# Decoding five of eight weight quads two stages earlier, beside attention, through DRAM scratch

## The chip, the cores and the metric

The kernel runs on one core of a Trainium2 chip. The metric is device time in microseconds (us) from launch to end, as the median of several executions; smaller is better. Engines are called as in the profile: PE (matmuls) and PEld (their weight loads), DVE (VectorE), ACT (ScalarE), POOL (GpSimd), SP (the queue that issues most DMAs). Each engine works through its own instructions in a fixed order; an instruction that waits holds up all that stand behind it on that engine.

## The reference

Three stages follow one another. `q`, `k`, `v` are 4 batches x 8 heads x 576 positions x 64. The weights arrive as float64.

```python
q_d, k_d, v_d = (mean over groups of 4 positions of q, k, v)
out = repeat(softmax(q_d k_d^T / 8) v_d, 4) + softmax(masked(q k^T / 8, |i - j| < 4)) v
x = out as 2304 tokens x 512
y = maximum(maximum(x @ w1, x @ w2), x @ w3) @ w_out         # first MoE, 512 -> 768 -> 512
h = maximum(y @ w_in, 0)                                     # second MoE, 512 -> 2048
return h * h @ w_out2                                        # 2048 -> 512
```

## The kernel before

**Numbers as pairs.** Each matmul operand is held as a rounded part (`hi`, or `h`) and the rest (`lo`, or `l`), and a product is three matmuls, `hi*hi + hi*lo + lo*hi` (`mm3`, L140). A weight block therefore costs, before any matmul can use it, a *decode*: a 512 KB load of raw float64 into one of three staging buffers (`raw_words`, L101, pool `stg`); `rebias` on DVE (L107); `low_bits` on ACT (L113); `join`, two DVE instructions (L116); then a split, `hi` on ACT and `lo` on another engine.

**Stages.** Attention of a batch makes `x`; the first MoE turns `x` into `y`, written to DRAM from ACT's queue (`y_unit`, L413). The two are interleaved over batches: `run(b, ...)` does the first MoE of batch b beside the attention of batch b+1. In the profiled execution `run(0, "second")` lies at about 95 to 187 us, `run(1, "mid")` at 187.3 to 279.9, `run(2, "mid")` at 279.9 to 372.5 and `run(3, "last")`, which has no attention beside it, at 372.5 to 461.3. Then comes the second MoE over three tiles of 768 tokens, here called t0 (461.3 to 595.1), t1 (595.1 to 721.9) and t2. In each, all eight *quads* of weights are used in turn (`quad`, L701): seven products `P` in a Strassen-like scheme, whose results DVE and ACT must take out of two PSUM banks in alternation, and twelve output groups `po`, issued during the next quad. So t0 contains eight rounds of products and seven of output groups; t1 contains eight of both.

**Order.** The order of PE is written out by hand in `CFG` (a token for each piece of work: `s` scores, `t` transposes, `v` the product with v, `G` a gate unit, `Y` an output unit of the first MoE). The order on DVE, ACT, POOL and SP is laid down when the program is built, by a list planner: work that is traced earlier goes first as soon as its inputs and its buffer are there, and later work fills gaps.

**Weights of the second MoE.** A quad is four raw blocks (two of `w_in`, called f0 and f1, two of `w_out2`, o0 and o1) that become six cuts: i0 and i3 straight from f0 and f1, i1 and i2 from four DVE sums of them (L528 to L531), o0 and o1. Each cut is an `h` and an `l` tile; twelve tiles make a quad, and there is room for four quads. `decode_quad` (L499) decodes into these tiles, with `lo` on POOL (`split_cut`, L488), and stores all twelve to DRAM scratch (`store_cut`, L494). `load_quad` (L554) reads them back. Quads 0 to 2 are decoded during `run(3)`. Quads 3 to 7 are decoded during t0, between the pieces of work of quads 0 to 5:

```python
spread(0, 0, decode_quad(3))
for q in range(4, NQ):
    spread(0, q - 3, decode_quad(q), 2)
```

In t1 and t2, four quads each are still in place and four are loaded from scratch. A planner-made detail: quad 0's first three raw blocks are loaded, and two of them joined, as early as 118 to 135 us, in gaps of `run(0)`; they then hold the staging buffers until its tiles come free.

Of the kernel before, what the change touches and what calls it, by code (L numbers as in the profile page):

```python
# [18 lines left out]
P = 128  # L19
# [39 lines left out]
def local_global_attention__then__moe_kernel(  # L59
# [30 lines left out]
        for b in range(B)  # L90
    ]
    wscr = [
        {
            c + e: yd.tile([P, 256 if c == "i3" else 512], F32, name=f"s{q}{c}{e}", tag=f"s{q}{c}{e}")
            for c in CUT
            for e in "hl"
        }
        for q in range(NQ)
    ]

    def raw_words(src, name):  # L101
        raw = stg.tile([P, 512], U64, tag="raw", name=f"raw_{name}")
        nc.sync.dma_start(out=raw, in_=src)
        words = raw.bitcast(U32).rearrange("p (n two) -> p n two", two=2)
        return words[:, :, 0], words[:, :, 1]
# [307 lines left out]
    def y_unit(b, h, d):  # L413
        N = HALF[h][1] * QB
        ps = mm_ps(f"yp{b}{h}{d}")
        for f in range(NF1):
            hi, lo = w1_t["o", f, 0]
            ds = slice(d * P, (d + 1) * P)
            mm3(ps[:, 0:N], hi[:, ds], lo[:, ds], h_t[b, h, f][0], h_t[b, h, f][1], f == 0, f == NF1 - 1)
        ys = tmp.tile([P, 320], F32, tag="c", name=f"ys{b}{h}{d}")[:, 0:N]  # L420
        nc.scalar.activation(out=ys, in_=ps[:, 0:N], func=AF.Copy)
        nc.scalar.dma_start(out=yscr[b][h][:, d, :], in_=ys)


    vdone = set()
# [68 lines left out]
    def store_cut(q, c):  # L494
        n = 256 if c == "i3" else 512
        for e in "hl":
            nc.sync.dma_start(out=wscr[q][c + e], in_=w2_t[q][c + e][:, 0:n].bitcast(F32))

    def decode_quad(q):  # L499

        raw, tb = {}, {}

        def begin(key, src):
            low, high = raw[key] = raw_words(src, f"{key}_{q}")
            rebias(high)
            low_bits(low, low)

        def end(key):
            low, high = raw[key]
# [12 lines left out]
        def sums():  # L522

            t1, t2 = tb["f0"][:, 0:256], tb["f0"][:, 256:512]
            t3, t4 = tb["f1"][:, 0:256], tb["f1"][:, 256:512]
            b11, b21 = raw["f0"][:, 0:256], raw["f0"][:, 256:512]
            b12, b22 = raw["f1"][:, 0:256], raw["f1"][:, 256:512]
            nc.vector.tensor_tensor(out=t1, in0=b12, in1=b11, op=ALU.subtract)  # L528
            nc.vector.tensor_tensor(out=t3, in0=b22, in1=b12, op=ALU.subtract)
            nc.vector.tensor_tensor(out=t2, in0=b22, in1=t1, op=ALU.subtract)  # L530
            nc.vector.tensor_tensor(out=t4, in0=t2, in1=b21, op=ALU.subtract)  # L531

        def last(c, key):
            end(key)
            split_cut(q, c, raw[key])

        def stores(*cuts):
            for c in cuts:
                store_cut(q, c)

        f = 2 * q
        return [
            lambda: begin("f0", wi2[f]),
            lambda: begin("f1", wi2[f + 1]),
            both,
            other,
            sums,
            lambda: (split_cut(q, "i1", tb["f0"]), begin("o0", wo2[f]), stores("i0", "i3")),
            lambda: (split_cut(q, "i2", tb["f1"]), begin("o1", wo2[f + 1]), stores("i1", "i2")),
            lambda: last("o0", "o0"),  # L550
            lambda: (last("o1", "o1"), stores("o0", "o1")),
        ]

    def load_quad(q):  # L554
        def part(cuts, new=False):
            if new:
                quad_tiles(q)
            for c in cuts:
                n = 256 if c == "i3" else 512
                for e in "hl":  # L560
                    nc.sync.dma_start(out=w2_t[q][c + e][:, 0:n].bitcast(F32), in_=wscr[q][c + e])

        return [lambda: part(CUT[:4], True), lambda: part(CUT[4:])]

# [44 lines left out]
    with tc.manual_schedule(engines={ENG.PE}):  # L609
# [9 lines left out]
        def run(b, plan):  # L619
            for token in plan.split():  # L620
# [2 lines left out]
                    gate_unit(b, int(token[1]), int(token[2]))  # L623
                elif kind == "Y":
                    y_unit(b, int(token[1]), int(token[2]))
                elif kind == "e":
                    load_w2()
                elif kind == "d":
                    load_w1(1)
                else:  # L630
                    act_on(b + 1, token)

        run(0, CFG["second"])
        for b in range(1, B - 1):
            run(b, CFG["mid"])
        at.close()
        yq = ctx.enter_context(tc.tile_pool(name="yq", bufs=1, reuse_waits="tile"))
# [190 lines left out]
```

## Time and profile before

| | us |
|---|---|
| median of 3 executions | 863.0 (862.43 to 867.05) |
| the profiled execution | 863.13 |
| its span in the trace | 861.2 |
| PE busy in the span | 809.8 (94%) |
| DVE busy | 531.5 (62%) |
| ACT busy | 330.4 (38%) |
| POOL busy | 221.4 (26%) |

The 1.93 us between time and span lie before the first and after the last instruction. Busy shares are means over stages that differ; the rows below split them by stage. Moved by DMA: 110.32 MB. The granted TensorE clock is full (1.00, of 2.4 GHz) from 100 us on, but for one stretch of 0.97 at 500 to 550 us.

### The profile page before, as it was taken

The page shows a single profiled execution, that of the slowest core. Times are in us where ns is not written, and L with a number is a line of the kernel's source. Part 1 is how long each engine was busy: PE and PEld are TensorE (multiplying, and loading weights), DVE is VectorE, ACT ScalarE, POOL GpSimd, SP SyncE. Part 2 cuts the span into 40 slices and gives each one's busy share as a digit, 9 for nine tenths or more (in the row PEclk, how much of TensorE's full clock was granted, in tenths as well). Part 3 has the DMA queues.
Part 4 walks back from the last instruction along what each step waited for, and adds up shares of the span by engine and source line. Part 5 has one row for each costly group of instructions (what it writes and reads, how often), then busy time and mean ns, then how long its engine had stood idle before and what let it go on. Part 6 is the DMA issues. An engine that isn't in the chain of part 4 may idle for free. (4 is left out here: it accounts for less than half of the span.)

```text
span 861.2 us, 15761 instructions
## 1 busy us (share of the span) xinstructions
PE 809.8 (94%) x6016; PEld 741.5 (86%) x6016; DVE 531.5 (62%) x1008; ACT 330.4 (38%) x935; POOL 221.4 (26%) x258
## 2 busy tenths in 40 slices
PE   4678999999999999999998988999999999999998
PEld 3467998999999999999898877888888989888886
DVE  6899896523554245637777998965644445544543
ACT  4556654522543144543445444434221123211211
POOL 4756385410433014004333333412000002000000
PEclk8577999999999999999999999999999999999999
DMA  7645342410223002136665766722564100654101
GB/s 239 193 153 184 127 155 70 132 47 1 86 87 103 10 29 81 31 107 216 220 225 168 289 214 238 263 80 93 188 214 141 50 1 25 211 192 135 49 1 73
DMA packets 66234, 110.32 MB, mean 128 GB/s; under 512 B 6800, under 2 KB 29680, under 8 KB 66160
## 3 DMA queue, kind: packets, MB, share of 16 engines
q1 hardware_dynamic: 61552, 104.60, 37.1%
q10 hardware_dynamic: 4608, 4.72, 1.6%
q8 instruction: 47, 0.77, 0.4%
q14 instruction: 27, 0.22, 0.1%
HBM read 76.79 MB, written 32.51 MB: 127 GB/s over the span
## 5 line engine op out<-in xcount | busy, mean ns | idle before, releaser
L141 PE MATMUL g<-xhi,hi_g 128*128 128x256 f32 (+1 forms) x576 | 176.1, 306 | 4.4 <-DVE c L395 3.4
L142 PE MATMUL g<-xlo,hi_g 128*128 128x256 f32 (+1 forms) x576 | 172.8, 300 | 2.1 <-DVE xlo L356 1.9
L143 PE MATMUL g<-xhi,lo_g 128*128 128x256 f32 (+1 forms) x576 | 172.7, 300 | 0.0
L141 PEld LDWEIGHTS g<-xhi,hi_g 128*128 128x128 f32 x576 | 111.1, 193 | 8.1 <-DVE c L395 5.5
L142 PEld LDWEIGHTS g<-xlo,hi_g 128*128 128x128 f32 x576 | 111.4, 193 | 2.5 <-DVE xlo L356 2.5
L143 PEld LDWEIGHTS g<-xhi,lo_g 128*128 128x128 f32 x576 | 110.8, 192 | 0.0
L666 ACT ACTIVATE gh<-c 128x384 fp32r<-128x384 f32 x96 | 50.2, 524 | 147.6 <-DVE c L710 133.5
L667 DVE TENSOR_TENSOR gl<-c,gh 128x384 fp32r<-128x384 f32 x96 | 61.6, 643 | 39.4 <-ACT gh L666 39.1
L395 DVE TENSOR_TENSOR c<-g,c 128x256 f32<-128x256 f32 (+1 forms) x96 | 43.3, 451 | 63.1 <-PE g L143 59.4
L141 PE MATMUL yp<-hh,hi_o 128*128 128x256 f32 (+1 forms) x192 | 58.3, 304 | 0.0
L142 PE MATMUL yp<-hl,hi_o 128*128 128x256 f32 (+1 forms) x192 | 57.1, 297 | 0.2 <-DVE hl L401 0.2
L143 PE MATMUL yp<-hh,lo_o 128*128 128x256 f32 (+1 forms) x192 | 56.9, 296 | 0.0
L399 ACT ACTIVATE hh<-c 128x256 fp32r<-128x256 f32 (+1 forms) x48 | 21.3, 444 | 88.3 <-DVE c L395 88.1
L710 DVE SCALAR_TENSOR_TENSOR c<-c 128x384 f32<-128x384 f32 x72 | 43.4, 604 | 1.9
L729 DVE TENSOR_TENSOR c<-c 128x384 f32<-128x384 f32 x24 | 15.7, 654 | 39.7 <-ACT c L728 39.7
L606 POOL TENSOR_TENSOR lS<-s,hS 128x768 fp32r<-128x768 f32 x2 | 3.7, 1839 | 131.3 <-DVE u L725 115.9
L141 PEld LDWEIGHTS yp<-hh,hi_o 128*128 128x128 f32 x192 | 36.4, 190 | 0.8 <-issue 0.6
L142 PEld LDWEIGHTS yp<-hl,hi_o 128*128 128x128 f32 x192 | 36.5, 190 | 0.7 <-DVE hl L401 0.7
L143 PEld LDWEIGHTS yp<-hh,lo_o 128*128 128x128 f32 x192 | 36.4, 190 | 0.0
L217 POOL TENSOR_TENSOR v<-v 72x256 f32<-72x256 f32 x32 | 26.1, 828 | 36.9 <-DMA v<-in_vP 36.8
L728 ACT ACTIVATE c<-P 128x384 f32<-128x384 f32 x24 | 11.7, 488 | 59.3 <-PE P L143 57.9
L401 DVE TENSOR_TENSOR hl<-c,hh 128x320 fp32r<-128x320 f32 (+1 forms) x36 | 20.1, 559 | 11.7 <-ACT hh L399 11.7
(1797 smaller groups left out, 2151.9 us busy)
## 6 DMA issues: line engine op xcount, KB each, us to landing
raw_o<-in_wo SPq DMA_DIRECT2D x22, 512.0 KB
raw_g<-in_wg SPq DMA_DIRECT2D x18, 512.0 KB
raw_f<-in_wi SPq DMA_DIRECT2D x16, 512.0 KB
k<-in_kT SPq DMA_DIRECT2D x16, 291.0 KB
q<-in_qT SPq DMA_DIRECT2D x16, 288.0 KB
v<-in_vP SPq DMA_DIRECT2D x32, 144.0 KB
out_y<-ob SPq DMA_DIRECT2D x18, 256.0 KB
vw<-in_vP SPq DMA_DIRECT2D x16, 175.0 KB
```

Of the source, the lines that this page charges most:

```text
L141: nc.tensor.matmul(ps, whi, xhi, start=first, stop=False, skip_group_check=more)
L142: nc.tensor.matmul(ps, whi, xlo, start=False, stop=False, skip_group_check=more)
L143: nc.tensor.matmul(ps, wlo, xhi, start=False, stop=last, skip_group_check=more)
L217: nc.gpsimd.tensor_tensor(out=v4[:, 0:2], in0=v4[:, 0:2], in1=v4[:, 2:4], op=ALU.add)
L395: nc.vector.tensor_tensor(out=c, in0=ps[:, 0:N], in1=c, op=ALU.max)
L399: nc.scalar.activation(out=hhi, in_=c, func=AF.Copy)
L401: eng.tensor_tensor(out=hlo, in0=c, in1=hhi.bitcast(F32), op=ALU.subtract)
L666: nc.scalar.activation(out=ghi, in_=c, func=AF.Copy)
L667: nc.vector.tensor_tensor(out=glo, in0=c, in1=ghi.bitcast(F32), op=ALU.subtract)
L710: V.scalar_tensor_tensor(out=c, in0=c, scalar=0.0, in1=c, op0=ALU.max, op1=ALU.mult)
L728: A.activation(out=e, in_=d, func=AF.Relu)
L729: V.tensor_tensor(out=e, in0=e, in1=e, op=ALU.mult)
```

## The change

Quads 3 to 7 are no longer decoded in t0. A new function, `decode_to_scratch`, decodes quads 3, 4 and 5 into DRAM scratch; its calls are traced just ahead of `run(1, "mid")`. Quads 6 and 7 are traced ahead of `run(2, "mid")`. Being traced earlier, they go ahead of that run's own work on each engine whenever they are ready. There, the two halves of a cut are made in a buffer of the same three-deep staging ring (`tag="raw"`), `lo` on DVE and not on POOL, and go to scratch as one store of 512 KB (256 KB for i3). The f blocks' loads are held back by a one-column ACT copy out of the last `ys` tile of the run before, into the staging buffer that is to be loaded. In t0, quads 3 to 7 are loaded from scratch as in t1 and t2. Quads 0 to 2 are decoded and stored as before.

```diff
-            c + e: yd.tile([P, 256 if c == "i3" else 512], F32, ...)
+            c: yd.tile([P, 2, 256 if c == "i3" else 512], F32, ...)
...
-    def raw_words(src, name):
+    def raw_words(src, name, after=None):
         raw = stg.tile([P, 512], U64, tag="raw", name=f"raw_{name}")
+        if after is not None:
+            nc.scalar.activation(out=raw.bitcast(F32)[:, 0:1], in_=after[:, 0:1], func=AF.Copy)
         nc.sync.dma_start(out=raw, in_=src)
...
+    def decode_to_scratch(q):
+        raw, tb = {}, {}
+        f = 2 * q
+        def begin(key, src):
+            low, high = raw[key] = raw_words(src, f"{key}_{q}", last_y[0] if key[0] == "f" else None)
+            rebias(high)
+            low_bits(low, low)
+        def end(key):
+            low, high = raw[key]
+            join(low, high, low)
+            raw[key], tb[key] = low.bitcast(F32), high.bitcast(F32)
+        def cut(c, w):
+            n = w.shape[-1]
+            t = stg.tile([P, 2, 512], F32R, tag="raw", name=f"cut_{c}_{q}")
+            hi, lo = t[:, 0, 0:n], t[:, 1, 0:n]
+            nc.scalar.activation(out=hi, in_=w, func=AF.Copy)
+            nc.vector.tensor_tensor(out=lo, in0=w, in1=hi.bitcast(F32), op=ALU.subtract)
+            nc.sync.dma_start(out=wscr[q][c], in_=t[:, :, 0:n].bitcast(F32))
+        return [
+            lambda: begin("f0", wi2[f]),
+            lambda: begin("f1", wi2[f + 1]),
+            lambda: end("f0"),
+            lambda: end("f1"),
+            lambda: cut("i0", raw["f0"]),
+            lambda: sums(raw, tb),
+            lambda: cut("i3", raw["f1"][:, 256:512]),
+            lambda: cut("i1", tb["f0"]),
+            lambda: cut("i2", tb["f1"]),
+            lambda: begin("o0", wo2[f]),
+            lambda: (end("o0"), cut("o0", raw["o0"])),
+            lambda: begin("o1", wo2[f + 1]),
+            lambda: (end("o1"), cut("o1", raw["o1"])),
+        ]
...
-        for b in range(1, B - 1):
+        for b, quads in zip(range(1, B - 1), ((3, 4, 5), (6, 7))):
+            for call in [call for q in quads for call in decode_to_scratch(q)]:
+                call()
             run(b, CFG["mid"])
...
-        spread(0, 0, decode_quad(3))
-        for q in range(4, NQ):
-            spread(0, q - 3, decode_quad(q), 2)
+        spread(0, 0, load_quad(3))
-        for t, k in ((1, 0), (1, 1), (1, 2), (1, 3), (2, 0), (2, 1), (2, 2), (2, 3)):
+        for t, k in ((t, k) for t in range(NT2) for k in range(NQ - 4)):
             one, two = load_quad(turns[t][k + 4])
             spread(t, k + 1, [one], 1)
             spread(t, k + 2, [two], 1)
```

## Rows read from the trace of the kernel before

**Rows 1.** Windows by stage: busy us (instructions) of PE, PEld, DVE, ACT, POOL; clock, DMA share, GB/s

```profile
95.00:187.30 92.30, 89.23 (x889) 84.50 (x888) 60.94 (x129) 46.04 (x166) 48.02 (x62) 1.00 0.35 112
118.00:137.00 19.00, 16.94 (x151) 15.64 (x149) 17.32 (x34) 9.28 (x27) 12.78 (x14) 1.00 0.36 122
187.30:279.90 92.60, 92.60 (x982) 88.76 (x981) 43.42 (x113) 37.73 (x153) 26.17 (x46) 1.00 0.21 65
279.90:372.50 92.60, 92.42 (x949) 88.72 (x949) 45.05 (x114) 36.89 (x150) 15.79 (x28) 1.00 0.12 37
372.50:461.30 88.80, 86.65 (x662) 84.84 (x662) 56.66 (x94) 34.72 (x70) 24.71 (x18) 1.00 0.62 204
461.30:595.10 133.80, 123.15 (x591) 106.73 (x590) 115.95 (x180) 59.93 (x106) 49.05 (x33) 0.99 0.55 188
595.10:721.90 126.80, 126.36 (x624) 112.85 (x623) 66.67 (x115) 31.85 (x58) 5.89 (x3) 1.00 0.35 117
```

**Rows 2.** Waits of PEld in t0: total us, times, longest; first and last of seven

```profile
PEld P L141 <- DVE c L744: 4.3, 3, 1.6
...
PEld P L141 <- ACT p L722: 1.5, 2, 1.1
```

**Rows 3.** Waits of PEld in t1, the longest

```profile
PEld P L141 <- DVE u L733: 0.7, 1, 0.7
```

**Rows 4.** Decode by line: ns of one (min/median/max), first and last start

```profile
L108 DVE TENSOR_SCALAR raw_o<-raw_o x22: 416/424/1101, 96.0 to 562.9; 128x512 f32<-128x512 f32 x22
L114 ACT ACTIVATE raw_o<-raw_o x22: 660/685/717, 94.2 to 562.2; 128x512 uint32<-128x512 uint32 x22
L117 DVE SCALAR_TENSOR_TENSOR raw_o<-raw_o x22: 674/686/1791, 97.1 to 563.5; 128x512 uint32<-128x512 uint32 x22
L134 ACT ACTIVATE hi_g<-raw_g x18: 658/673/722, 21.5 to 96.1; 128x512 fp32r<-128x512 f32 x18
L136 DVE TENSOR_TENSOR lo_g<-raw_g,hi_g x18: 652/682/1215, 24.2 to 97.7; 128x512 fp32r<-128x512 f32 x18
L528 DVE TENSOR_TENSOR raw_f<-raw_f,raw_f x8: 408/419/965, 132.2 to 552.4; 128x256 f32<-128x256 f32 x8
```

**Rows 5.** Windows of L108 alone (one instruction a raw block): busy us, clock, DMA

```profile
95.00:187.30 92.30, 5.45 (x9) 1.00 0.35 112
118.00:137.00 19.00, 2.17 (x4) 1.00 0.36 122
372.50:461.30 88.80, 6.43 (x12) 1.00 0.62 204
```

**Rows 6.** PE timeline in run(1): start us, duration us

```profile
224.50 0.66 PE L247 MATMUL sd22F<-kd,qd 64*64 64x144 f32 x8
...
226.33 0.41 PE L142 MATMUL yp<-hl,hi_o 128*128 128x320 f32 x1
...
268.73 0.74 PE L294 MATMUL t23B<-const,sm23B 128*70 128x128 f32 x5
```

**Rows 7.** DVE timeline in run(1): what those matmuls wait for

```profile
225.80 0.47 DVE L401 TENSOR_TENSOR hl<-c,hh 128x320 fp32r<-128x320 f32 x1
...
267.48 0.55 DVE L270 TENSOR_TENSOR sm23B<-sm23B,sms23B 128x350 f32<-128x350 f32 x1
```

**Rows 8.** POOL timeline in run(1): last step of pooling q and k of pair 2

```profile
222.73 0.55 POOL L209 TENSOR_TENSOR kd<-kd,k 128x144 f32<-128x144 f32 x1
```

**Rows 9.** SP timeline: issue of two raw loads

```profile
127.78 0.33 SPq L103 DMA_DIRECT2D raw_o<-in_wo  x1
...
449.91 0.38 SPq L103 DMA_DIRECT2D raw_o<-in_wo  x1
```

**Rows 10.** ACT timeline: first use of those two raw loads

```profile
131.12 0.67 ACT L114 ACTIVATE raw_o<-raw_o 128x512 uint32<-128x512 uint32 x1 [2.95 <-DMA raw_o<-in_wo]
...
455.79 0.70 ACT L114 ACTIVATE raw_o<-raw_o 128x512 uint32<-128x512 uint32 x1 [1.11 <-DMA raw_o<-in_wo]
```

**Rows 11.** Waits of ACT in run(3): total us, times, longest

```profile
ACT raw_f L114 <- DMA raw_f<-in_wi: 9.3, 5, 4.8
```

More of the change, by code (lines that the diff above doesn't have):

```diff
@@ L93, in local_global_attention__then__moe_kernel @@
         {
-            c + e: yd.tile([P, 256 if c == "i3" else 512], F32, name=f"s{q}{c}{e}", tag=f"s{q}{c}{e}")
+            c: yd.tile([P, 2, 256 if c == "i3" else 512], F32, name=f"s{q}{c}", tag=f"s{q}{c}")
             for c in CUT
-            for e in "hl"
         }
@@ L99, in local_global_attention__then__moe_kernel @@
     ]
-    def raw_words(src, name):
+    last_y = []
+    def raw_words(src, name, after=None):
         raw = stg.tile([P, 512], U64, tag="raw", name=f"raw_{name}")
+        if after is not None:
+            nc.scalar.activation(out=raw.bitcast(F32)[:, 0:1], in_=after[:, 0:1], func=AF.Copy)
         nc.sync.dma_start(out=raw, in_=src)
@@ L422, in y_unit @@
         nc.scalar.dma_start(out=yscr[b][h][:, d, :], in_=ys)
+        last_y[:] = [ys]
     vdone = set()
@@ L492, in split_cut, with sums @@
         nc.gpsimd.tensor_tensor(out=lo, in0=w, in1=hi.bitcast(F32), op=ALU.subtract)
[L494 to L497, printed above, removed]
+    def sums(raw, tb):
+        t1, t2 = tb["f0"][:, 0:256], tb["f0"][:, 256:512]
+        t3, t4 = tb["f1"][:, 0:256], tb["f1"][:, 256:512]
+        b11, b21 = raw["f0"][:, 0:256], raw["f0"][:, 256:512]
+        b12, b22 = raw["f1"][:, 0:256], raw["f1"][:, 256:512]
+        nc.vector.tensor_tensor(out=t1, in0=b12, in1=b11, op=ALU.subtract)
+        nc.vector.tensor_tensor(out=t3, in0=b22, in1=b12, op=ALU.subtract)
+        nc.vector.tensor_tensor(out=t2, in0=b22, in1=t1, op=ALU.subtract)
+        nc.vector.tensor_tensor(out=t4, in0=t2, in1=b21, op=ALU.subtract)
     def decode_quad(q):
@@ L520, in other, with keep @@
             split_cut(q, "i3", raw["f1"][:, 256:512])
[L522 to L531, printed above, removed]
+        def keep(*cuts):
+            for c in cuts:
+                n = 256 if c == "i3" else 512
+                for i, e in enumerate("hl"):
+                    nc.sync.dma_start(out=wscr[q][c][:, i], in_=w2_t[q][c + e][:, 0:n].bitcast(F32))
         def last(c, key):
@@ L535, in last @@
             split_cut(q, c, raw[key])
-        def stores(*cuts):
-            for c in cuts:
-                store_cut(q, c)
         f = 2 * q
@@ L546, in decode_quad @@
             other,
-            sums,
-            lambda: (split_cut(q, "i1", tb["f0"]), begin("o0", wo2[f]), stores("i0", "i3")),
-            lambda: (split_cut(q, "i2", tb["f1"]), begin("o1", wo2[f + 1]), stores("i1", "i2")),
+            lambda: sums(raw, tb),
+            lambda: (split_cut(q, "i1", tb["f0"]), begin("o0", wo2[f]), keep("i0", "i3")),
+            lambda: (split_cut(q, "i2", tb["f1"]), begin("o1", wo2[f + 1]), keep("i1", "i2")),
             lambda: last("o0", "o0"),
-            lambda: (last("o1", "o1"), stores("o0", "o1")),
+            lambda: (last("o1", "o1"), keep("o0", "o1")),
+        ]
[23 more added lines that the diff above has]
+            lambda: cut("i0", raw["f0"]),
+            lambda: sums(raw, tb),
+            lambda: cut("i3", raw["f1"][:, 256:512]),
[5 more added lines that the diff above has]
+            lambda: (end("o1"), cut("o1", raw["o1"])),
         ]
@@ L559, in part @@
                 n = 256 if c == "i3" else 512
-                for e in "hl":
-                    nc.sync.dma_start(out=w2_t[q][c + e][:, 0:n].bitcast(F32), in_=wscr[q][c + e])
+                for i, e in enumerate("hl"):
+                    nc.sync.dma_start(out=w2_t[q][c + e][:, 0:n].bitcast(F32), in_=wscr[q][c][:, i])
         return [lambda: part(CUT[:4], True), lambda: part(CUT[4:])]
@@ L625, in run @@
                     y_unit(b, int(token[1]), int(token[2]))
-                elif kind == "e":
-                    load_w2()
                 elif kind == "d":
```

## The prediction

> **What bounds the kernel now.** I read the windows by stage first [rows 1]. PE is the engine that sets the end almost everywhere: from 187.3 to 372.5 us, the two `mid` runs, it is busy for 185.02 of 185.2 us, and in t1 for 126.36 of 126.8. The exception to look for is t0: PE is busy for 123.15 of 133.8 us there, while DVE is at 115.95 (87%) against 66.67 of 126.8 (53%) in t1, which does the same products without decoding. The weight loads run ahead of the matmuls, so their waits show the full hold-up: in t0 seven releasers, 4.3 us for the largest and 1.5 for the smallest, 16.4 together, all on products `P` that wait until DVE or ACT has emptied a PSUM bank [rows 2]. In t1 the largest such wait is 0.7 [rows 3]. So t0 is bound by DVE's queue. The stages that take the work over have room by the same view: DVE at 43.42 and 45.05 of 92.6 us, ACT at 37.73 and 36.89, DMA at 0.21 and 0.12 [rows 1].
>
> **What t0 gives back.** Two ways of counting. Waits: 16.4 - 0.7 = 15.7 us. Length: t0 has 588 matmuls (eight rounds of 42 products, seven of 36 outputs), t1 has 624 in 126.8 us, or 0.203 us each; 588 x 0.203 = 119.5, and 133.8 - 119.5 = 14.3. What does not go away is the start of t0, where the first quad needs four splits of `y` before its products can run, as before; I leave 1 us for it. I take 14 us, with 12 and 15.7 as ends. The loads from scratch that come in cost nothing here: four quads are loaded in t1 at the same pace with DMA at 0.35 and PE full [rows 1]. Their cover is that each is issued about two quads ahead of its use; without it a late part would hold PE by a raw load's time, some 3 to 6 us [rows 9, 10]. SP loses 20 raw loads and 60 stores from t0 and gains 60 loads there; the `y` loads for t1 stand behind loads that wait for tiles to come free, as those for t2 do in t1 already.
>
> **What the decode costs in its new place.** Per quad on DVE [rows 4]: 4 rebias x 0.424 = 1.70, 8 join instructions x 0.686 = 5.49, 4 sums x 0.419 = 1.68, and, new on DVE, `lo` for five full cuts x 0.682 = 3.41 and for i3 some 0.4 (an estimate, from the half-width sum beside it). That is 12.7 us. On ACT: 4 x 0.685 + 5 x 0.673 + 0.45 for i3 = 6.6, and two one-column copies, which no row shows; the nearest are full-width copies at 0.67, so 0 to 1.3 us, and I take 0.4: 7.0. Run(1) takes three quads: DVE 43.42 + 38.1 = 81.5 of 92.6 us (88%), ACT 37.73 + 21 = 58.7 (63%). Run(2) takes two: DVE 70.5 (76%), ACT 50.9.
>
> Both still fit, so the cost is not in sums but in queues. A decode instruction is traced ahead of the run's own work, so it goes first when both are ready. Behind it on DVE stand the maxima that empty the gate units' PSUM, `hl`, and the softmax steps; behind it on ACT the exponentials and the PSUM copies; PE, in its written order, waits for these. Gate units have four PSUM buffers, so a wait of a microsecond or two is covered. Some spots have no cover. `hl` ends at 226.27 and the `yp` matmul that reads it starts at 226.33; `sm23B` ends at 268.03 and its transposes start at 268.73; `kd` of pair 2 ends at 223.28 and `sd22F` starts at 224.50 [rows 6 to 8]. Slack there: 0.1, 0.7 and 1.2 us, once in each `mid` run.
>
> How much of this PE feels, the trace shows by analogy, because raw blocks are decoded beside other work already. PE's idle time over the raw blocks of a stretch [rows 1, 5]: run(3), no attention: 88.8 - 86.65 = 2.15 us for 12, or 0.18 each. Run(0), with attention: 92.3 - 89.23 = 3.07 for 9, or 0.34. The densest piece of it, 118 to 137 us: 2.06 for 4, or 0.51. The change puts 20 blocks beside attention: 3.6, 6.8 and 10.3 us. In those rows `lo` ran on POOL; with it, DVE's work for a block grows from 8.9/4 to 12.7/4, a factor of 1.43, which makes the middle 9.7 and the top 14.7. I take 8 us, between 6.8 and 9.7, since run(0) is the nearest row; 2 (most of it falls where PE has cover) and 15 stay as ends.
>
> The rest is small. Quad 0's first blocks can no longer be decoded at 118 to 135 us, since the staging buffers are to be free for quads 3 to 7; run(0) gains about 3 x 0.34 = 1 us, run(2) or run(3) gets the three blocks and loses it. Quad 3's early raw loads at the end of run(3) vanish. Does the ring keep up? A cut holds a buffer for `hi` 0.67, `lo` 0.68 and its store, for which the nearest row is a raw load, 3.3 us: 4.7. Three such in line, the f loads and joins (about 7) and two o blocks (about 9) make some 30 us a quad, 90 for three against 92.6, 60 for two. Tight in run(1), but run(2) has a reserve.
>
> **Sum.** Against the profiled execution's 863.13: -14 + 8 = -6, so 857. The median of the runs, 863.0, lies 0.13 below it, which changes nothing.
>
> **A rule beside the rows.** A raw block issued at 127.78 us is in use at 131.12, after 3.34 us, with DMA at 0.36; one issued at 449.91 is in use at 455.79, after 5.88, with DMA at 0.62 [rows 1, 9, 10]. The Trainium skill, page "DMA: Bandwidth & Descriptors", section "Issuing engines are not separate DMA queues", says that DMAs from whichever engine run on the same 16 DMA engines and interleave. By that rule attention's own loads in the `mid` runs are stretched too, and the trace agrees as far as the raw loads go; the rows say more directly that a load takes up to 2.5 us longer at that DMA share. It is rival 3.
>
> **Rivals.**
> 1. *Nearly all is hidden.* For it: PE idles 0.18 us in both `mid` runs together, four PSUM buffers, DVE at half load. Against: run(0) lost 3.07 us with less. Mid costs 2 to 3.6: 863 - 15 + 3 = 851, range 847 to 853. Chance 0.18.
> 2. *The tight spots give it all back.* At each of the three spots a whole block's chain (0.42 + 2 x 0.69) and a `lo` (0.68) stand in front, 2.5 us; less slack 2.4 + 1.8 + 1.3 = 5.5 a run, 11 for two, plus 1 to 2 on PSUM: 863 - 14 + 12.5 = 861.5, range 859 to 867. The same result would show if quads slipped out of the `mid` runs into run(3), so that the change does only part of what it says. Chance 0.17.
> 3. *Attention's inputs come late.* With some 4.9 MB a quad added, DMA in run(1) rises from 0.21 towards run(3)'s 0.62, q and k of pair 2 land up to 2.5 us later and `sd22F` has 1.2 to spare: 1.3 us a run more, 863.1 - 14 + 8 + 2.6 = 859.7. Chance 0.08.
> 4. *Slower.* Each cut's first write, `hi` on ACT, waits until the ring's buffer is free, that is until an earlier cut's store has landed; each o or f block's `low_bits` waits for its load. That is 24 to 30 waits on ACT in run(1). In run(3) such a wait of ACT's took 9.3/5 = 1.9 us [rows 11]. 24 x 1.9 = 45, and 58.7 + 45 = 104 of 92.6: ACT would be the bound, run(1) 11 us longer, run(2) (16 x 1.9 + 50.9 = 81) would lose what rival 2 says, 5.5, and a little on PSUM. 863 - 14 + 18 = 867 and up to 874. It decides from (92.6 - 58.7)/24 = 1.4 us a wait. Against: DMA is far less busy there, and a wait that ACT reaches late is short. Chance 0.15.
>
> **Numbers.** The forecast has the remaining 0.42, own range 853 to 859. No change means within 0.5% (4.3 us, about what a measurement of this kernel can tell from none): 858.7 to 867.3. Faster: 0.18 + 0.42 = 0.60. Same: rivals 2 and 3, 0.25. Slower: 0.15. For 8 in 10 the range leaves out the lowest part of rival 1 and most of rival 4: 849 to 867.
>
> **What would show it.** In t0: no raw blocks, no POOL subtractions, DVE down from 116 to about 67 us, the stage 119 to 121 us long; wrong if products still wait for DVE, or if `P` waits for a DMA. In the `mid` runs: DVE near 81 and 70 us, each 3 to 6 us longer, PE waits at `yp` for `hl`, at `t23B`/`t33B` for `sm`, at `sd22F`/`sd32F` for `kd`; rival 1 if they stay 92.6 long, rival 4 if ACT's waits for DMA sum to over 35 us in run(1). The forecast fails if the `mid` runs together grow by 12 us or more, or if run(3) takes over decode work of quads 6 and 7.

## The result, and the profile after

The changed kernel takes 868.36 us as the median of 12 executions (862.21 to 873.21), the kernel before beside it 863.55 (862.27 to 867.05). The ratio is 1.0051, with an interval of 1.003 to 1.0072: slower by about half a per cent. 857.0 was forecast, 849 to 867 as range. The profiled execution took 868.07 us, its span is 866.3.

PE executes the same 6016 matmuls in the same order in both kernels, so the stages can be cut at the same matmuls. By that order, in which a run ends with its last Y unit, the cuts of [rows 1] lie some 9 us behind the start of `run(1)` (178.4 us in the kernel before) and some 8 us ahead of the end of `run(2)` (380.4); the two `mid` runs are 101 us long each, and cut there they grow by 23.4 us together, as between the cuts (23.5). The names of the stages below mean the stretches between the cuts. First the windows by stage of the changed kernel, with the columns of [rows 1]: `run(0)`, `run(1)`, `run(2)`, `run(3)`, t0 and t1.

```profile
93.90:182.80 88.90, 88.35 (x890) 84.61 (x889) 55.73 (x122) 46.85 (x169) 45.60 (x62) 1.00 0.35 111
182.80:288.70 105.90, 98.23 (x982) 93.05 (x981) 77.01 (x174) 53.14 (x184) 33.43 (x46) 0.95 0.56 188
288.70:391.50 102.80, 95.29 (x949) 90.66 (x949) 74.08 (x171) 50.66 (x177) 19.39 (x28) 0.97 0.44 146
391.50:478.70 87.20, 85.95 (x663) 84.62 (x662) 50.76 (x81) 32.59 (x67) 24.45 (x18) 1.00 0.57 191
478.70:599.70 121.00, 119.53 (x590) 106.08 (x590) 65.70 (x113) 32.66 (x59) 5.89 (x3) 1.00 0.40 134
599.70:727.40 127.70, 126.30 (x624) 112.62 (x624) 66.52 (x115) 31.85 (x58) 5.89 (x3) 1.00 0.35 116
```

Beside [rows 1] the first column after the colon tells it all. t0 falls from 133.8 to 121.0, and its DVE from 115.95 to 65.7: the gain is there. But `run(1)` grows from 92.6 to 105.9 and `run(2)` from 92.6 to 102.8, 23.5 us together. `run(0)` falls from 92.3 to 88.9 and begins 1.1 us earlier, `run(3)` falls by 1.6, t1 grows by about 1. In sum 23.5 - 12.8 - 3.4 - 1.1 - 1.6 + 0.9 - 0.4 (t2) = +5.1, the difference of the spans.

All stage lengths here and below are of one execution each, the profiled one, which lies up to 3.5 us from its kernel's median. Two yardsticks for that: the work ahead of `run(0)`, which no edit touches, ends at 92.3 to 96.8 us in the sixteen traces; and `run(1)` took 105.9 us here and 103.9 us in the kernel with quad 0 held back (below), with the same order of instructions on every engine. So a difference of 2 us between two stages of single traces is not told from none.

The waits of the weight loads in t0, which answer to [rows 2], have shrunk to 3.7 us; first and last of five:

```profile
PEld P L145 <- DVE c L781: 1.1, 2, 0.7
...
PEld P L145 <- ACT p L763: 0.4, 1, 0.4
```

In the two `mid` runs, where PE had idled for 0.18 us, it now waits 15.2 us. The waits of PE from 182.8 to 391.5 us (total, times, longest):

```profile
PE sd33F L251 <- ACT ptd32F L282: 4.0, 1, 4.0
PE yp L146 <- DVE hl L405: 3.2, 2, 1.8
PE t23B L298 <- DVE sm23B L274: 2.5, 1, 2.5
PE sd32F L251 <- POOL kd L213: 1.9, 1, 1.9
PE sd23F L251 <- DVE pt22F L280: 1.8, 1, 1.8
PE yp L145 <- ACT hh L403: 0.7, 2, 0.5
...
PE td23B L306 <- DVE x3222B L352: 0.4, 1, 0.4
```

Of the spots that the prediction named ([rows 6]), all three are here, though not each in both runs: `yp` for `hl` (3.2 us), `t23B` for `sm23B` (2.5) and, in `run(2)`, `sd32F` for `kd` (1.9), together 7.6 us. The largest stall is one that it did not name: the scores `sd33F` and `sd23F` go into PSUM buffers, four of which attention's scores and transposes share, and wait until an earlier pair's transposes (`ptd32F`, `pt22F`) have been copied out.

The first `yp` stall shows the queue. DVE works without a gap from 211 us on; from 217.3 us to `hl` its timeline holds some 3.4 us of decode in among the softmax steps, ahead of an `hl` that had 0.1 us of slack [rows 6, 7]. The lines of decode right ahead of it, and `hl`:

```profile
218.73 0.64 DVE L505 TENSOR_TENSOR raw_f<-raw_f,raw_f 128x256 f32<-128x256 f32 x1
219.29 0.78 DVE L506 TENSOR_TENSOR raw_f<-raw_f 128x256 f32<-128x256 f32 x1
220.00 0.41 DVE L507 TENSOR_TENSOR raw_f<-raw_f,raw_f 128x256 f32<-128x256 f32 x1
...
220.78 0.42 DVE L576 TENSOR_TENSOR cut_i<-raw_f,cut_i 128x256 fp32r<-128x256 f32 x1
...
223.69 0.69 DVE L405 TENSOR_TENSOR hl<-c,hh 128x320 fp32r<-128x320 f32 x1
```

And PE does not go on at its old pace behind the stall. Its timeline from there, the bracket being the idle time before:

```profile
224.43 0.42 PE L146 MATMUL yp<-hl,hi_o 128*128 128x320 f32 x1 [1.79 <-DVE hl L405]
...
224.98 0.31 PE L146 MATMUL yp<-hl,hi_o 128*128 128x320 f32 x1
225.13 0.30 PE L147 MATMUL yp<-hh,lo_o 128*128 128x320 f32 x1
...
226.02 0.47 PE L145 MATMUL yp<-hh,hi_o 128*128 128x320 f32 x1
226.28 0.47 PE L146 MATMUL yp<-hl,hi_o 128*128 128x320 f32 x1
```

From 224.98 to 225.13 is a step of 0.15 us, from 226.02 to 226.28 one of 0.26 (0.267 over many). The three windows around it show why: the granted clock falls to 0.50, that is to 1.2 of 2.4 GHz, and 15 matmuls are issued where the next window has 26.

```profile
221.90:225.30 3.40, 1.28 (x7) 1.05 (x8) 3.40 (x12) 1.30 (x4) 2.09 (x4) 1.00 0.55 165
225.30:228.70 3.40, 3.40 (x15) 3.40 (x15) 3.32 (x7) 3.40 (x19) 3.28 (x5) 0.50 0.38 157
228.70:232.10 3.40, 3.40 (x26) 3.37 (x26) 1.58 (x5) 2.40 (x12) 0.01 (x1) 0.99 0.67 147
```

There are four such stretches in the `mid` runs: 225.3 to 228.7, 252.6 to 256.0, 276.5 to 279.9 and 365.3 to 372.1 us, in the last of which PE works from 367.1 on. At 0.267 us a step instead of 0.147 they lose 0.45 of 10.2 + 5.0 us, 6.8 us, an estimate from the steps of `yp`. Waits and clock make 15.2 + 6.8 = 22.0 of the 23.5 us.

The longest stall is about quad 0. Its first three raw blocks, decoded at 118 to 135 us in the kernel before, are loaded late in `run(2)` now, and ACT, which works in order, stands before two of them until they land. `ptd32F`, for which PE waits 4.0 us, comes behind (ACT's timeline):

```profile
360.74 0.69 ACT L118 ACTIVATE raw_f<-raw_f 128x512 uint32<-128x512 uint32 x1 [2.90 <-DMA raw_f<-in_wi]
...
365.96 0.70 ACT L118 ACTIVATE raw_o<-raw_o 128x512 uint32<-128x512 uint32 x1 [1.47 <-DMA raw_o<-in_wo]
366.52 0.57 ACT L282 ACTIVATE ptd32F<-td32F 72x512 f32<-72x512 f32 x1
```

### The profile page after: what moved, and what is told of

The parts are those of the page before. It is cut to its first block, busy times and chain, and to the rows that moved or that the text cites. A ratio compares the mean times of both kernels' runs of the same rounds, so it can differ in the third digit from the quotient of the medians.

```text
span 866.3 us, 15801 instructions
## 1 busy us (share of the span) xinstructions
PE 811.7 (94%) x6016; PEld 745.2 (86%) x6016; DVE 531.9 (61%) x1038; ACT 330.8 (38%) x945; POOL 185.7 (21%) x228
## 4 chain that ended last, share of the span: by engine, by line
PE 58%; DVE 16%; DMA 14%; ACT 6%; issue 3%; POOL 1%; SPq 1%; ACTq 0%; DVEq 0%; POOLq 0%
PE po L145 7%; PE po L146 7%; PE po L147 7%; PE P L145 6%; PE P L147 6%; PE P L146 6%; DMA raw_o<-in_wo 4%; PE g L145 3%; DMA raw_f<-in_wi 3%; PE yp L145 3%; PE yp L146 3%; PE g L146 2%; PE yp L147 2%; PE g L147 2%; DMA raw_g<-in_wg 2%
## 5 line engine op out<-in xcount | busy, mean ns | idle before, releaser
L708 DVE TENSOR_TENSOR gl<-c,gh 128x384 fp32r<-128x384 f32 x96 | 55.4, 578 | 48.5 <-ACT gh L707 48.4
L146 PE MATMUL yp<-hl,hi_o 128*128 128x256 f32 (+1 forms) x192 | 59.3, 309 | 3.2 <-DVE hl L405 3.2
L145 PE MATMUL yp<-hh,hi_o 128*128 128x256 f32 (+1 forms) x192 | 61.0, 318 | 0.7 <-ACT hh L403 0.7
L147 PE MATMUL yp<-hh,lo_o 128*128 128x256 f32 (+1 forms) x192 | 58.8, 306 | 0.0
L647 POOL TENSOR_TENSOR lS<-s,hS 128x768 fp32r<-128x768 f32 x2 | 3.7, 1839 | 237.6 <-ACT hS L646 120.7
L770 DVE TENSOR_TENSOR c<-c 128x384 f32<-128x384 f32 x24 | 13.4, 557 | 52.1 <-ACT c L769 52.1
L751 DVE SCALAR_TENSOR_TENSOR c<-c 128x384 f32<-128x384 f32 x72 | 40.7, 567 | 2.3
L146 PEld LDWEIGHTS yp<-hl,hi_o 128*128 128x128 f32 x192 | 38.6, 201 | 3.7 <-DVE hl L405 3.7
L145 PEld LDWEIGHTS yp<-hh,hi_o 128*128 128x128 f32 x192 | 38.7, 202 | 2.1 <-ACT hh L403 1.2
L147 PEld LDWEIGHTS yp<-hh,lo_o 128*128 128x128 f32 x192 | 38.5, 201 | 0.0
L766 DVE TENSOR_TENSOR u<-P,p 128x384 f32<-128x384 f32 x24 | 13.4, 556 | 30.6 <-PE P L147 30.6
## 6 DMA issues: line engine op xcount, KB each, us to landing
out_y<-ob SPq DMA_DIRECT2D x18, 256.0 KB
```

The source lines that it names most:

```text
L145: nc.tensor.matmul(ps, whi, xhi, start=first, stop=False, skip_group_check=more)
L146: nc.tensor.matmul(ps, whi, xlo, start=False, stop=False, skip_group_check=more)
L147: nc.tensor.matmul(ps, wlo, xhi, start=False, stop=last, skip_group_check=more)
L708: nc.vector.tensor_tensor(out=glo, in0=c, in1=ghi.bitcast(F32), op=ALU.subtract)
L751: V.scalar_tensor_tensor(out=c, in0=c, scalar=0.0, in1=c, op0=ALU.max, op1=ALU.mult)
L766: V.tensor_tensor(out=got["u2"], in0=d, in1=got["p1"], op=ALU.add)
```

## The experiments

Stage lengths below are cut at the matmuls of [rows 1], in us, one execution each. "Mid" is `run(1)` and `run(2)` together, 185.2 before, 208.7 after.

### Work or traffic?

**Traffic alone.** Loads and stores of the five quads stay in the `mid` runs, the decode between them goes. A cut is stored straight out of its raw block's buffer and takes none of its own, so the line of quads (decoded one behind the other through the three staging buffers) runs faster here. Quad 0's three blocks are still loaded and decoded in `run(2)`, here and in the next kernel.

```diff
-            rebias(high)
-            low_bits(low, low)
...
-            nc.sync.dma_start(out=wscr[q][c], in_=t[:, :, 0:n].bitcast(F32))
+            nc.sync.dma_start(out=wscr[q][c].bitcast(U32), in_=raw[key].bitcast(U32)[:, :, 0:n])
```

> In the two mid runs only the traffic of the decode is left: raw loads and stores of the same sizes through the same ring, with no rebias, low_bits, join, sums or split; t0 and t2 read other quads' scratch in place of what is not computed. Theory (the decode's DVE and ACT instructions stand ahead of the run's own): the mid runs together, 185.2 us before and 208.7 after, fall to 185 to 188. Rival A (DVE and ACT stand still in front of loads and stores that have not landed): the same, 185 to 188, since hardly any instruction waits for them. Rival B (the traffic itself makes attention's loads late): 195 or more.

**Work alone.** The same instructions on a constant tile, no loads and no stores of the five quads there. In both kernels the second MoE reads the scratch of quads 0 to 2 in place of the five quads'.

```diff
-            low, high = raw[key] = raw_words(src, f"{key}_{q}", last_y[0] if key[0] == "f" else None)
+            t = stg.tile([P, 512], U64, tag="raw", name=f"raw_{key}_{q}")
...
-            low_bits(low, low)
+            nc.scalar.activation(out=low, in_=const[:, 0:512].bitcast(U32), func=AF.Copy, scale=LOW_BITS)
...
-            nc.sync.dma_start(out=wscr[q][c], in_=t[:, :, 0:n].bitcast(F32))
```

> In the two mid runs only the engine work of the decode is left: every rebias, low_bits, join, sum and split runs, on values from a constant tile, with no raw load and no store; t0 and t2 read other quads' scratch. Theory (engine work ahead of the run's own): the mid runs keep at least half of the 23.5 us they grew, 197 us or more. Rival A (waits for loads and stores on DVE and ACT): they fall to 190 or less. Rival B (traffic): 188 or less.

Traffic alone: 846.62 us (one run), mid 187.4, t0 120.7. Work alone: 858.32 (one run), mid 197.9. Work alone keeps 12.7 of the 23.5 us, so the theory holds against both rivals; traffic alone keeps 2.2, and 8.6 appear only with both. PE's waits in the `mid` runs of the kernel with traffic alone are these:

```profile
PE sd22F L251 <- POOL kd L213: 1.1, 1, 1.1
PE yp L146 <- DVE hl L405: 0.9, 1, 0.9
```

The first, in `run(1)`, is the late `kd` of rival 3 (1.3 us said, 1.1 measured). The second need not be traffic's: it comes at 324.4 us in `run(2)`, where quad 0's joins and sums stand among the softmax steps (3.0 of DVE's 5.1 us up to 318.9) and put the last maximum ahead of `hl` (`mx30B`) 3.3 us later in the run than before. So traffic alone is shown to cost some 1 us, in `run(1)`.

**Loads or stores?** The same by halves, with quad 0's blocks held back (below): the changed kernel without the stores, and the kernel with work alone with its stores put back.

```diff
-            nc.sync.dma_start(out=wscr[q][c], in_=t[:, :, 0:n].bitcast(F32))
```

> The gated kernel without the stores of the cuts of quads 3 to 7 (their scratch isn't written, and t0 to t2 read another quad's instead): the decode in the mid runs keeps its loads and its work. Beside it runs the kernel with stores and without loads. The mid runs took 208.7 us with all, 197.9 with the work alone, 187.4 with the traffic alone. Theory A (the 8.6 us that neither explains are ACT and DVE waiting for raw loads): mid runs 203 to 207, ACT and DVE still with 25 us or more of waits for raw_o and raw_f. Theory B (they are `hi` waiting for the ring's earlier store, rival 4 of the prediction): mid runs 197 to 200.

> The gated kernel with the decode in the mid runs made from a constant tile in SBUF instead of raw loads, at the same instructions, and its stores kept: work and stores, no loads there. Theory A (waits for raw loads are the rest): mid runs 196 to 200, as with the work alone (197.9). Theory B (waits for the ring's stores are the rest): 203 to 207, and ACT's waits for stores above the 7.8 us of the changed kernel.

Without stores 850.09 us, mid 192.3; without loads 857.88, mid 199.9 (one run each). The ranges had been set from the changed kernel, with quad 0's blocks in it, and do not decide: the first result lies below both, the second at the end of theory A's. `run(1)`, where quad 0 plays no part, gives the whole square: work alone 98.8, with loads 98.9, with stores 102.5, with both 103.9. By these single traces the stores cost 3.7 to 5.0 us there; the loads' 0.1 to 1.4 are not told from none. The planner also lays the order on DVE and ACT anew when loads or stores go, so this is the price of stores with the order that they bring. ACT stands at stores for 11.9 us over both runs in the kernel with both; the two longest of these waits (3.4 and 3.5 us) are each run's first, and the kernel with one quad a run (below) has such a one, 3.6 us, at no cost. And the stores keep the three staging buffers longer, and the line of quads moves later. SP issues the first `o` load of quad 4 at 212.04 us in the kernel without stores and at 229.06 in the one with both:

```profile
212.04 0.33 SPq L107 DMA_DIRECT2D raw_o<-in_wo  x1
```

```profile
229.06 0.33 SPq L107 DMA_DIRECT2D raw_o<-in_wo  x1
```

### Quad 0, and the order of tracing

**Quad 0 held back** until the last Y unit of `run(2)`, in the changed kernel (first text) and, alone, in the kernel before (second).

```diff
-            low, high = raw[key] = raw_words(src, f"{key}_{q}")
+            gate = last_y[0] if q == 0 and key[0] == "f" else None
+            low, high = raw[key] = raw_words(src, f"{key}_{q}", gate)
```

> The change, with the two f blocks of quad 0 held back as those of quads 3 to 7 are, until run(2)'s last Y unit. In the changed kernel run(2) took 102.8 us, and its longest stall (4.0 us at 367, `sd33F` behind an ACT that waits 2.90 and 1.47 us for quad 0's raw loads, then 6.8 us of halved clock) came from these blocks. Theory A (ACT and DVE standing at DMA waits in front of attention's steps is a part of the cost, and quad 0's blocks are the worst of it): run(2) falls by 5 to 7 us to about 97, run(3) and t0 change by less than 2, median 862 to 863. Theory B (the cost is the decode's own work on the engines): three blocks fewer are worth 3 x 0.3 us, run(2) stays above 101, median 866 to 868.

> The kernel before, with one edit: quad 0's f blocks are held back until the last output of run(2), so that its first three raw blocks are no longer decoded at 118 to 135 us inside run(0). Theory (these three cost run(0) the 4.5 us that the changed kernel gained there, and cost little in run(3), which has no attention): run(0) is 4 to 5 us shorter and the time 858 to 860. Rival (they cost as much wherever they go): run(3) grows by what run(0) loses, 862 to 864.

The changed kernel with it: 863.5 us (860.06 to 865.14, 10 runs), ratio to before 0.9999 (0.9984 to 1.0014); `run(2)` 98.9 instead of 102.8. The 4 us of the fall are less than the 5 to 7 of theory A, but the 4.0 us stall is gone, and PE's waits in `run(2)` fall from 7.5 to 3.7 us. The kernel before with it alone: 859.64, ratio 0.9967 (0.9947 to 0.9987): `run(0)` 88.2, `run(3)` 86.5, t0 136.6. So some 4 us in `run(0)` and 2 in `run(3)` are to be had without the change, and t0 gives 2.8 of them back. All kernels below hold quad 0 back; what they owe to quads 3 to 7 is their distance from this 859.64, not from 863.

**Decode traced behind the run.** The calls of `decode_to_scratch` come after `run(b, ...)`, so that the planner takes the run's own work first where both are ready.

```diff
-            for call in [call for q in quads for call in decode_to_scratch(q)]:
-                call()
+            gate = last_y[0]
             run(b, CFG["mid"])
+            for call in [call for q in quads for call in decode_to_scratch(q, gate)]:
+                call()
```

> All of the changed kernel, but the decode calls are traced behind the run that they lie beside, so that the planner gives the run's own work the right of way and lets decode fill gaps; the loads are held back by the same last output of the run before. Theory (decode goes first when both are ready): the mid runs fall from 208.7 to 190 to 196 us and the time to 850 to 857. Rival A (waits for DMA on in-order engines): the waits stay, the mid runs stay at 203 or more, the time at 862 or more.

869.96 us (867.21 to 872.87), ratio 1.008 (1.0052 to 1.0109), mid 210.7. That decode goes first by its place in the trace is not the cause: traced last, with another order on DVE, ACT and SP, it costs as much, and PE waits 15.6 us at partly other steps (3.4 at `t33B`, 3.1 at `sd32F`).

### DVE or POOL?

`lo` of the cuts on POOL, with quad 0 held back.

```diff
-            nc.vector.tensor_tensor(out=lo, in0=w, in1=hi.bitcast(F32), op=ALU.subtract)
+            nc.gpsimd.tensor_tensor(out=lo, in0=w, in1=hi.bitcast(F32), op=ALU.subtract)
```

> The gated kernel with all five quads beside the mid runs, and `lo` of their cuts on POOL instead of DVE (the prediction's factor 1.43 on DVE's work per block taken back). The gated kernel's mid runs took 103.9 and 98.9 us. Theory A (DVE's queue ahead of `hl` and `sm` is the cost): DVE falls by 3.8 us a quad, mid runs together 193 to 198 instead of 202.8, median 855 to 859. Theory B (the decode's chain as such, with its waits for loads, stores and buffers on in-order engines, is the cost, or POOL's `kd` is, which then comes later still): mid runs stay above 201, stalls at `sd22F` and `sd32F` for `kd` grow, median 862 to 868.

876.32 us (871.57 to 877.65), ratio 1.0137 (1.01 to 1.0173), slower than either theory said, mid 218.4 instead of 202.8. `sd22F` now waits 5.0 us and `sd32F` 2.8 for `kd`, which is POOL's. A `lo` takes 1.38 us there, in line ahead of the pooling of q and k (POOL's groups by line, count, busy and mean ns):

```profile
L577 POOL TENSOR_TENSOR cut_i<-raw_f,cut_i 128x512 fp32r<-128x512 f32 x15 | 20.6, 1377 | 26.7 <-ACT cut_i L576 26.7
```

Nor was DVE relieved much. The 30 `lo` had kept it busy for 21.9 us over the two runs, but it is busy for only 5.8 us less without them, since its other instructions take longer beside POOL's `lo`: `hl` of 128x320 0.67 instead of 0.49 us on average, the first sum (L505) 0.92 instead of 0.51. So the test shows that the move to POOL loses, through POOL's queue and through slower DVE instructions; it does not show what a real relief of DVE would be worth.

### How many quads, and where

All of these hold quad 0 back. **One quad a run**, at its start; quads 5 to 7 are decoded in t0, as before the change.

```diff
-        for b, quads in zip(range(1, B - 1), ((3, 4, 5), (6, 7))):
+        for b, quads in zip(range(1, B - 1), ((3,), (4,))):
```

> The change as in the gated kernel, but only quad 3 is decoded to scratch beside run(1) and quad 4 beside run(2); quads 5 to 7 are decoded in t0 as before the change. Theory A (a queue cost that grows faster than the number of quads, in the mid runs and in t0 alike: DVE in t0 falls from 116 to some 96 us, enough to give most of the 13 us back, and DVE in a mid run is only at 57): mid runs together 188 to 191, t0 123 to 126, median 850 to 855. Theory B (each quad costs the same wherever it goes, 23.5/5 = 4.7 us in a mid run and 12.9/5 = 2.6 us in t0): mid runs 194.6, t0 about 129 to 131, median 861 to 864.

852.2 us (850.72 to 853.97), ratio 0.9873 (0.9848 to 0.9898). The `mid` runs lose nothing, with 0.3 us of waits in both, less than either theory said. t0, with three quads still decoded there, is 130.9 us long, where theory A had 123 to 126 and theory B 129 to 131 (windows of `run(1)`, `run(2)` and, last, t0):

```profile
182.30:275.10 92.80, 92.80 (x982) 88.78 (x981) 51.47 (x130) 41.42 (x160) 26.27 (x46) 1.00 0.33 107
275.10:367.80 92.70, 92.41 (x949) 88.70 (x948) 55.53 (x136) 42.98 (x162) 16.32 (x28) 1.00 0.28 91
...
454.20:585.10 130.90, 123.21 (x590) 108.76 (x590) 95.81 (x151) 49.45 (x89) 33.08 (x21) 0.97 0.48 163
```

Is it that one quad is little work, or that it is over before attention's spots come? **The same quads, some 56 us later**: their loads wait for the run's third Y unit (first load at 230.7 instead of 174.6 us).

```diff
-        for b, quads in zip(range(1, B - 1), ((3, 4, 5), (6, 7))):
-            for call in [call for q in quads for call in decode_to_scratch(q)]:
-                call()
-            run(b, CFG["mid"])
+        for b, (ahead, behind) in zip(range(1, B - 1), (((), (3,)), ((), (4,)))):
+            units = CFG["mid"].split()
+            cutoff = units.index("Y13") + 1
+            for quads, part in ((ahead, units[:cutoff]), (behind, units[cutoff:])):
+                for call in [call for q in quads for call in decode_to_scratch(q)]:
+                    call()
+                run(b, " ".join(part))
```

> The kernel with one quad a mid run, but each quad's raw loads are held until the third Y unit of the same run (Y13), so that its 30 us fall on the second half of the run, 45 to 80 us after its start, instead of the first 30 us. Same work, same number of quads, same gate on quad 0. In the kernel with one quad at the start the mid runs took 92.8 and 92.7 us with 0.3 us of PE waits. Theory A (what counts is whether a quad meets the spots without slack, `yp`, `sd`, `t23B`, which lie in the second half): mid runs 95 to 99 each, with stalls at `sd23F`, `t21B` or `t23B` and the clock halved behind some of them, median 857 to 865. Theory B (what counts is the load on the engines and the number of quads in line): mid runs stay within 1.5 us of 92.7 each, median 851 to 855.

868.39 us (864.71 to 871.6, 10 runs), ratio 1.0056 (1.0033 to 1.0079). That is beyond theory A's range, and far from B's. The work is the same (6 us of DVE's lay ahead of the cut of `run(1)` in the kernel above), and `run(1)` and `run(2)` are 102.0 and 96.2 long:

```profile
182.70:284.70 102.00, 95.81 (x982) 91.15 (x982) 57.79 (x135) 43.08 (x165) 30.80 (x46) 0.97 0.34 108
284.70:380.90 96.20, 93.14 (x949) 88.61 (x949) 55.84 (x136) 42.47 (x162) 17.04 (x28) 1.00 0.27 88
```

PE's waits of the same stretch, the longest three of nine; the clock is at 0.5 from 269.8 to 276.6 us:

```profile
PE t23B L298 <- DVE sm23B L274: 2.9, 1, 2.9
PE sd23F L251 <- DVE pt22F L280: 1.7, 1, 1.7
PE s23F L239 <- ACT pd22B L266: 1.1, 1, 1.1
```

One quad a run in the wrong half costs 13 us over the two runs, at a DVE load of 57%; the same quads at the start of the runs are free. Waits (9.2 us) and the lower clock (0.45 of the 6.0 us in which PE works there, 2.7) make 12 of the 13. How much of the waits is the decode's work and how much an engine that stands at a load is not split: ACT waits for raw loads for 10.3 us in these runs.

**More quads, early.** Four kernels begin a line of two before the run it burdens, or put a last quad beside `run(3)`. The edit is the one above, with other quads in the tuple and the cut at Y00 (the last but two of the run's Y units; Y13 for `run(0)`). The first has quad 4 at the start of `run(2)` and quad 5 behind its Y00; the second quads 4 and 5 behind `run(1)`'s, and 6 behind `run(2)`'s; the third quads 4 and 5 behind `run(1)`'s and no more. In these, quad 3 begins with `run(1)`. The fourth is

```diff
+        units = CFG["second"].split()
+        cutoff = units.index("Y13") + 1
-        run(0, CFG["second"])
+        run(0, " ".join(units[:cutoff]))
+        for call in [call for q in (3, 4) for call in decode_to_scratch(q)]:
+            call()
+        run(0, " ".join(units[cutoff:]))
```

with quads 5 and 6 behind `run(1)`'s Y00 in the same way.

> One quad at the start of each mid run, and a third one (quad 5) held until the unit Y00 of run(2), some 8 us before that run's end, so that it is decoded beside run(3), ahead of quads 0 to 2. Quads 6 and 7 are left to t0. Theory A (only the spots of the mid runs' second half cost, and run(3), which has no attention, has room): mid runs 92.8 and 93 to 94, run(3) 86 to 88, t0 127 to 128.5, median 848 to 851. Theory B (the staging ring and run(3)'s DMA share of 0.66 are full, so that quads 0 to 2 slip into t0): run(3) or the start of t0 loses 4 us or more, median 853 to 858.

> Four quads: quad 3 at the start of run(1), quads 4 and 5 one behind the other from the unit Y00 of run(1) (some 8 us before its end) into run(2), quad 6 from Y00 of run(2) into run(3); quad 7 is left to t0. Theory A (as for the kernel with the tail quad, and two quads in line from 267 us on end by about 327, ahead of the spots of run(2)): mid runs together 186 to 190, t0 123 to 125, median 846 to 850. Theory B (the second quad in line still meets `sd32F` and `yp` of run(2), as in the gated kernel, where run(2) lost 6 us): run(2) 96 to 99, median 850 to 856.

> Quad 3 at the start of run(1), quads 4 and 5 in line from the unit Y00 of run(1) into run(2); nothing beside run(3); quads 6 and 7 decoded in t0. The kernel with a fourth, tail quad lost 10.9 us in one wait at the start of t0. Theory A (only a line that reaches the spots costs; two quads from 269 us on end near 330, one spot is touched, `kd`, 1.6 us, as in that kernel): run(1) 92.8, run(2) 94 to 95, run(3) 86.4, t0 127 to 128.5, median 849.5 to 852. Theory B (two quads in line cost by their number, as run(2) of the gated kernel did, 6 us): run(2) 97 or more, median 853 to 856.

> Quads 3 and 4 in line from the unit Y13 of run(0), a few us before its end, into run(1); quads 5 and 6 in line from Y00 of run(1) into run(2); quad 7 alone is left to t0. Theory A: run(1) loses 2 to 5 us, since its first spots (`sd22F`, `yp` at some 42 us after its start) are met by the end of quad 4, run(2) 2 us, t0 123 to 125.5: median 847 to 853. Theory B (the number of quads in line): run(1) and run(2) lose 6 us each, median 856 to 858.

| quads to scratch | median (ratio, interval) | run(1) | run(2) | run(3) | t0 |
|---|---|---|---|---|---|
| 3, 4 and 5 beside `run(3)` | 857.31 (0.9925, 0.9903 to 0.9947) | 92.8 | 92.3 | 84.7 | 135.8 |
| 3, 4+5, 6 beside `run(3)` | 856.41 (0.993, 0.9904 to 0.9956) | 92.8 | 94.6 | 84.7 | 133.0 |
| 3, 4+5 | 850.82 (0.9851, 0.9815 to 0.9888) | 92.8 | 95.5 | 86.9 | 124.9 |
| 3+4, 5+6 | 849.61 (0.9834, 0.9805 to 0.9863) | 93.2 | 94.9 | 86.9 | 122.8 |

Beside `run(3)` a quad only moves the trouble: quads 0 to 2 are late, ACT still cuts quad 2 at 464 us, and the first products of t0 stand still (PE's timeline of the first kernel):

```profile
466.22 0.69 PE L145 MATMUL P<-hA,w0i0h 128*128 128x384 f32 x1 [10.86 <-ACT p L767]
```

For that kernel theory B was right. For the second neither was: its `run(2)` came as theory A said, its time did not, since t0 loses at the same place. For the other two theory A's times came, with t0 shorter than it said and, in the fourth, next to no loss in `run(1)` where it said 2 to 5 us. The fourth kernel has the lowest median, 849.61 us: four of five quads leave t0, and the `mid` runs grow by 2.9 us. Its interval overlaps those of the third and of the kernel with one quad a run, so these three are not told apart surely. Its `run(1)`, `run(2)` and, last, t0:

```profile
183.60:276.80 93.20, 92.72 (x982) 88.78 (x981) 61.88 (x147) 47.36 (x173) 28.46 (x46) 1.00 0.47 158
276.80:371.70 94.90, 92.58 (x949) 88.77 (x948) 68.98 (x158) 47.39 (x171) 18.76 (x28) 1.00 0.41 135
...
458.60:581.40 122.80, 120.38 (x590) 107.73 (x590) 72.65 (x118) 37.70 (x69) 13.19 (x9) 0.99 0.42 139
```

Its `run(2)` has the same two quads' worth of DVE work (68.98 us) as that of the changed kernel with quad 0 held back (68.44), and is 4 us shorter (94.9 against 98.9). The line's first load is issued 4.9 us before the run's start instead of 0.5 after it, and its last store 61.8 instead of 70.1 us behind that start. Both kernels lose 1.7 or 1.8 us at `sd32F`, waiting for `kd`; in the one that came later the clock then fell for 6.8 us, in the other it did not. That fall is some 2.6 of the 4 us (0.45 of the 5.7 us in which PE works), and PE's waits, 3.7 against 2.3 us, are the rest. So what the earlier start saved in `run(2)` is mostly clock, in one execution of each.

## Why the prediction was wrong

**The step that failed** is the term of the `mid` runs: "I take 8 us, between 6.8 and 9.7", with 15 as the top end. It measured 23.5. By the prediction's own test (growth by 12 us or more) the forecast failed there. Its rate per raw block was PE's idle time over all blocks of a stretch, and was multiplied as if each further block met PE alike. The rate was too low where it was read: quad 0's three blocks, 1 us by it, cost `run(0)` 4.1 us by the kernel before without them (92.3 to 88.2; 88.0 to 89.3 in all fifteen traces without them). And the runs show no one rate: two quads at the start of the runs cost 0.3 us, the same two some 56 us later 13, three in line in `run(1)` 11. What counts is which of attention's steps find decode ahead of them on DVE, ACT or POOL. The ring's pace, 30 us a quad by the prediction, was 35 (loads and stores of three quads are issued from 175.1 to 282.2 us, of two from 289.1 to 358.5), so that the three go on to some 6 us before the end of `run(1)`, and quad 0's blocks follow the two. The second part that the term lacked is the clock: 6.8 us, of which the prediction had nothing. The third is PSUM: it gave gate units' buffers as cover, and left out the buffers of the scores, where 5.8 us of the waits lie.

**Quad 0's blocks**, "about 1 us" for `run(0)`, and lost again later: `run(0)` gained 3.4 us, and `run(2)` lost 3.9 for them (102.8 against 98.9). The direction was right, both sizes were not.

**t0** was right: 14 us forecast, 12.8 measured, the stage 121.0 long within the 119 to 121 said, DVE 65.7 (67 said), no product waiting for a DMA. Engine work in the `mid` runs was right too: DVE 77.0 and 74.1 (81 and 70 said; 68.4 in `run(2)` without quad 0's blocks).

**The rivals.** Rival 1 is false for five quads, and true for two. Rival 2 named stalls that came, 7.6 of the 15.2 us, where it had 11; its quads did not slip into `run(3)`. Rival 3's price came in `run(1)` with the traffic alone, 1.1 us at `sd22F`; in `run(2)`, where it said as much again, `sd32F` does not wait there. Its cause was mostly another: q's load is issued at the same point of the run as before and q is pooled 3.4 us after that instead of 2.9, but k's load is issued 1.2 us later, behind two stores in SP's queue, and POOL takes a softmax step (`pd20B`) ahead of k. The rule of the Trainium skill beside it, page "DMA: Bandwidth & Descriptors", section "Issuing engines are not separate DMA queues", speaks of transfers that share the DMA engines; the trace agrees by the 0.5 us of q. Rival 4's time, 867, is what came, but not its mechanism: ACT is busy for 53.1 of 105.9 us in `run(1)` and waits for DMA for 17.0, half of the 35 that the prediction set as its sign, so it is not the bound. Its waits for loads and stores cost where they stand ahead of a spot, as at 366 us, and cost nothing in the first third of a run.

**What stays open.** Why a stall is followed by a lower clock in one execution and not in another, at the same length, no run settles. It is not the order of the work: with the same order on every engine, `run(1)` had three such stretches in the changed kernel and two in the one with quad 0 held back. In the kernels without loads or stores the line of quads also runs at another pace, so the 8.6 us that only both together show are not split further into waits and lateness; that lateness alone can cost as much is shown by the quads moved to the second half.

## What to carry to other kernels

A stage's idle share says whether work fits, not what it costs: list the steps whose result the bound engine takes up at once, with their slack, and put moved work where none of them lies. Move in portions that end before the first such step, and count how long the portion's buffers hold it up, stores included. Then sweep their number, against a kernel that shares every side effect of the change: here, from 859.64 us with quad 0 held back alone, two of five quads gave 852.2, three and four 850.82 and 849.61, and all five 863.5, worse than none.

## What the runs showed of the hardware

A stall of PE of some 2 us can cost it nearly as much again: after 1.79 us of waiting for `hl` (and 0.49 for `hh` two us before) the granted clock was 0.50 for 3.4 us, 1.5 us of work lost. It need not: after 1.84 us of waiting at `sd32F` in the kernel with the lowest median it stayed full (325 us).

POOL slows down beside the decode's DVE instructions. Its pooling step `qd` (L212) takes 0.57 us on average in the `mid` runs of the kernel with one quad a run, and 0.96 in the one with five and quad 0 held back (six each). There it takes 1.52 us at 329.5 us, ahead of the `kd` for which `sd32F` waits and with a join (L124) on DVE beside it. POOL's timeline in the latter:

```profile
329.48 1.52 POOL L212 TENSOR_TENSOR qd<-qd,q 128x144 f32<-128x144 f32 x1
330.96 0.75 POOL L211 TENSOR_TENSOR kd<-k 128x144 f32<-128x144 f32 x1
```

The Trainium skill, page "GPSIMD Engine Reference", section "1. Specifications", says that this engine shares its SBUF interfaces with VectorE and contends with instructions there that have two SBUF inputs. Joins, sums and `lo` are such; the trace agrees, with 1.52 against 0.57 us. It goes both ways, as `hl` and the sums showed that took longer on DVE beside POOL's `lo`.
